# Query features of the first two batches made directly with features on partitions, and their product on quarters of the array

## The chip, the cores and the metric

The kernel runs on one core of one Trainium2 chip. The metric is device time in microseconds (us), the median of several runs; lower is better. The engines are named as in the profile: PE (TensorE products), PEld (its weight loads), DVE (VectorE), ACT (ScalarE), POOL (GpSimd) and SP (SyncE, which here issues DMAs).

## The reference

Two blocks follow each other. The first is a sketched attention over 4 batches, 4 heads, 1088 tokens and head size 32, with r = 8:

```python
def phi(x):
    a = np.einsum('rd,bhsd->bhsr', S1, x)
    b = np.einsum('rd,bhsd->bhsr', S2, x)
    return np.einsum('bhsi,bhsj->bhsij', a, b).reshape(*x.shape[:-1], r * r)
q_p, k_p = (phi(q), phi(k))
kv = np.einsum('bhsf,bhsd->bhfd', k_p, v)
z = np.sum(k_p, axis=2)
num = np.einsum('bhsf,bhfd->bhsd', q_p, kv)
den = np.einsum('bhsf,bhf->bhs', q_p, z)[..., None] + 1e-06
out = num / den
```

Every query and key of 32 numbers becomes 64 features, all products of its 8 + 8 sketches. The second block takes the 4352 tokens of 128 numbers (four heads side by side), sends each to one of 8 experts by cosine similarity with a softmax gate, and gives it that expert's two layers (128 to 1024, relu, 1024 to 128).

## The kernel before

All arithmetic is in 32-bit floating point except small counting tables. The four batches are worked on as two pairs, m = 0 and m = 1; the two batches of a pair lie side by side. Tokens come in tiles of 128; a pair has 17 tiles (the last one, the "rest", holds what is left of both batches), taken as four groups: three of 4 tiles and a last one of 4 + 1.

The order of the work is written out by hand. Each step of work is put into a numbered tick with a rank (`put(after, rank, f)`: tick of the group plus `after`), and `emit` issues all steps by tick and rank; each engine then runs its instructions strictly in that order. The keys of m = 0 take ticks 0 to 3, those of m = 1 ticks 4 to 7. The queries of m = 0 are made in ticks 0 to 3, and multiplied with the keys' sums in ticks 4 to 7; m = 1 follows in ticks 8 to 11. From tick 9 on the experts' blocks are interleaved, one a tick, with the rest of the attention and with the tables that say which token goes to which block.

What the change and the prediction touch, with the names in the code:

- `turned` (L346) turns 4 tiles of keys or queries by four products with the identity (L354) and copies the result from PSUM (L356, ScalarE). The result `kT` or `qT` has on its partitions 4 tiles x 32 head numbers, and in its columns 4 heads x 128 tokens.
- `sketch` (L362) multiplies with the block-diagonal sketch matrix `Sblk` in eight products (L371), which brings the tokens back to the partitions: the 8 + 8 sketches of every token and head. In ticks 0 to 3 keys and queries share one buffer of two PSUM banks (`ps_big`), later each has one bank (`ps_ab`).
- `second` (L375) copies one half of the sketches to SBUF (`kb`, `qb`, L377), and `features` (L380) makes the 64 products on VectorE (L383), 1024 columns for 4 tiles. For the queries of m = 0 they are kept in `held`, a part of the space of `w2_sb` that is loaded only later.
- `kv` (L420) sums keys' features times values over all tiles in PSUM (L432). At the end `total` (L438) copies the sums to SBUF: once as `kv` (L440) and twice into `kz` (L443), which holds for each pair of heads a block-diagonal 128 x 82 matrix, cleared beforehand by POOL (`clear`, L302). `tr_kv`, `kvT` and `kve` add to `kz` the sums already multiplied with the experts' directions (L447, L451, L455, L459).
- `tr_qp` (L504) is the second turn: eight more products with the identity (L508) put the queries' features on partitions, two heads x 64, and `qpT` (L512) copies them to SBUF (L514, ScalarE, 1024 columns). For m = 0 this is done one or two ticks before their use.
- `nd` (L516) multiplies `qpT` with `kz`: 16 products a group (L522), 128 rows by 64 of the array's columns, 82 moving columns, into `ps_big`. The two halves of 64 tokens go to the two halves of the array's columns.
- `x` (L529) divides by the denominator and sums the experts' parts on VectorE (L532 to L539); `squares` (L541) makes the norms on ScalarE (L544) and POOL (L546).
- `router` (L597) picks the expert and writes the tokens' rows to DRAM (`write`, L660, and on POOL L666); `fetch` (L858) gathers blocks of rows (L861), `up` and `down` are the two layers (L917, L943), with weights copied on VectorE (L874).

PSUM has two buffers of one bank (`ps_t`), two of two banks (`ps_big`), and one bank each for `ps_acc` and `ps_ab`. A step that needs a buffer waits until all readers of its last use are done. SP issues the loads in the order of the program, at most eight of them under way at a time: q, k and v of the pairs, then the experts' weights; the writes of rows and the late part of `w2_sb` follow in the same queue.

Of the kernel before, what the change touches and what calls it, by code (L numbers as in the profile page):

```python
# [19 lines left out]
P = 128  # L20
# [43 lines left out]
def kernel(  # L64
# [25 lines left out]
    def ps_big():  # L90
        return psum.tile([P, 2, 512], F32, tag="big", bufs=2, name="ps_big")
# [130 lines left out]
    nc.vector.tensor_mul(Sblk, bview(ST, [[0, H], [1, 2 * R]]), bview(mask4, [[1, H], [0, 2 * R]]))  # L222

    half_c = consts.tile([P, SPAN], F32, name="half_c")
    nc.gpsimd.memset(half_c, 0.5)
# [70 lines left out]

    kz = [consts.tile([P, 2, 2, 2, COLS], F32, name=f"kz{m}") for m in range(NM)]

    en_blk = consts.tile([P, 4, 2, E], F32, name="en_blk")

    def clear(m):
        nc.gpsimd.memset(kz[m], 0.0)  # L302

# [75 lines left out]

    def features(ab, b, n, tag, t=None):  # L380
        if t is None:
            t = tile_of(n, [P, n, H, R * R], tag)
        nc.vector.tensor_mul(t.rearrange("p j h (i k) -> p (j h) i k", i=R),  # L383
                             ab[:, :, 0].unsqueeze(3).broadcast_to([P, n * H, R, R]),
                             b.unsqueeze(2).broadcast_to([P, n * H, R, R]))
        return t

    def ab_bank(tick, n, u):


        if (tick, n) not in ab_ps:
            if tick >= 2 * n_g and n == 1:
                ps = ab_ps[tick, 4][:, 1:]
            elif n == 1:
                ps = ps_small()[:, :2 * n * HALF].rearrange("p (u n) -> p u n", u=2)
            elif tick < n_g:
                ps = ps_big()
            else:

                ps = ps_one("acc" if tick == 2 * n_g + 1 else "ab").rearrange("p (u n) -> p u n", u=2)  # L400
            ab_ps[tick, n] = ps
        return ab_ps[tick, n][:, u, :n * HALF]

    def keys(m, c0, c1, put):
# [33 lines left out]
        def total():  # L438
            s["kv"] = work.tile([P, 2, 2, D], F32, tag="kv", bufs=1, name="kv")
            nc.scalar.copy(s["kv"], acc[m][:, :, :, :D])  # L440
            for u in range(2):
                r = slice(u * HALF, (u + 1) * HALF)
                nc.scalar.copy(kz[m][r, :, :, u, :D + 1], acc[m][r, :, :, :D + 1])  # L443

# [8 lines left out]
        def kve():  # L453
# [3 lines left out]
            for u in range(2):  # L457
                r = slice(u * HALF, (u + 1) * HALF)
                nc.scalar.copy(kz[m][r, :, :, u, D + 1:], ps[r, :, :, u])  # L459
# [18 lines left out]
    def queries(m, c0, c1, put, put_nd):  # L478
# [21 lines left out]
        def prod():  # L500
            t = held[:, c0 // 4].rearrange("p (j h f) -> p j h f", j=4, h=H) if m == 0 and n > 1 else None
            s["qp"] = features(s["ab"], s["b"], n, "qp", t)

# [12 lines left out]
        def nd():  # L516
            ps = ps_big().rearrange("p b (u n) -> p (b u) n", u=2) if n > 1 else ps_small().unsqueeze(1)
            W = 2 * COLS
            for j in range(n):
                for p in range(2):  # L520
                    for i in range(2):
                        nc.tensor.matmul(  # L522
                            ps[i * HALF:(i + 1) * HALF, j, p * W:(p + 1) * W],
                            s["qpT"][:, p, j * P + i * HALF:j * P + (i + 1) * HALF],
                            kz[m][:, i if n == 1 else c0 // NK, p].rearrange("p h d -> p (h d)"), start=True, stop=True)
            s["hs"] = ps[:, :n, :2 * W].rearrange("p n (h d) -> p n h d", h=H)
            spare[m, c0] = ps[:, 0, 2 * W:]

        def x():  # L529
            hs = s["hs"]  # L530
            rc = work.tile([P, 4, H], F32, tag="rc", name="rc")[:, :n]
            nc.vector.tensor_scalar_add(rc, hs[:, :, :, D], DEN_EPS)  # L532
            nc.vector.reciprocal(rc, rc)
            nc.vector.tensor_mul(xg[g][:, own, :DM].rearrange("p n (h d) -> p n h d", h=H), hs[:, :, :, :D],  # L534
                                 bview(rc, [[H, n], [1, H], [0, D]]))

            t = work.tile([P, 4, H, E], F32, tag="parts", bufs=1, name="parts")[:, :n]
            nc.vector.tensor_mul(t, hs[:, :, :, D + 1:], bview(rc, [[H, n], [1, H], [0, E]]))
            nc.vector.reduce_sum(out=lg[g][:, own], in_=t.rearrange("p n h e -> p n e h"), axis=AX.X)  # L539

# [559 lines left out]
```

## Time and profile before

| | us |
|---|---|
| median of 9 runs | 212.23 |
| lowest and highest run | 211.31, 215.24 |
| profiled execution, whole | 211.22 |
| its span, first to last instruction | 209.3 |

The profiled execution lies about 1 us below the median. Its span is 1.9 us shorter than its whole time. The granted clock of TensorE is 1.00 in it.

Reading it: a group line gives the source line, engine, operation, tiles (out<-in), shape, then the busy time, the mean ns of one instruction and the idle time of the engine before it. A 32-bit product is recorded as two MATMUL and two LDWEIGHTS instructions; a turn as one of each. The durations of single products overlap, as they are pipelined; their rate is read from the time from the first start to the last. In the windows each row gives its stretch and length, then busy us and instruction count for PE, PEld, DVE, ACT and POOL, the granted clock, the DMA engines' share and GB/s.

The groups of the stage in question, for orientation (busy us, mean ns):

| group | count | busy | mean |
|---|---|---|---|
| L508 PE, second turn of m = 0 | 32 | 4.3 | 278 |
| L514 ACT, its copy (both pairs) | 8 | 8.1 | 1007 |
| L522 PE, features times kz (both pairs) | 256 | 10.9 | 236 |
| L371 PE, sketch of q in ticks 0 to 3 | 64 | 2.6 | 225 |
| L383 DVE, features of q, m = 0 | 4 | 4.9 | 1213 |
| L356 ACT, copy of 512 columns | 8 | 4.7 | 587 |
| L534 DVE, product of 512 columns from PSUM | 8 | 5.5 | 691 |

### The profile page before, as it was taken

To read this page: it belongs to the slowest core of one execution; us is meant where nothing else is said; L and a number is where in the kernel's file an instruction comes from. 1 tells how busy PE (TensorE), PEld (TensorE's weight loads), DVE (VectorE), ACT (ScalarE), POOL (GpSimd) and SP (SyncE) were. 2 spreads that over 40 slices of the span, in tenths; PEclk is the share of its full clock that TensorE was granted. 3 is DMA by queue.
4 is the path that set the end of the run, shared out by engine and by line. 5 is a ranking of instruction groups with operands and counts; after the bars stand their busy time and mean duration, and the time that the engine had idled before them with its cause. 6 is when DMAs were issued, how large, how long until landed. Compare 5 with 4: busy or idle time off the path is not lost.

```text
span 209.3 us, 6754 instructions
## 1 busy us (share of the span) xinstructions
PE 196.3 (94%) x2566; PEld 186.4 (89%) x2566; DVE 127.6 (61%) x368; ACT 106.0 (51%) x288; POOL 107.6 (51%) x116
## 2 busy tenths in 40 slices
PE   8979999987889999999999999999999999999991
PEld 7758889966778989998999999999999999999990
DVE  5975576898988777888554454534535356575300
ACT  2544477675569745363334535344353534676430
POOL 4101002163278786731678777676766767751322
PEclk9999999999999999999999999999999999999999
DMA  4989889999720302300111111111011121110000
GB/s 121 310 213 303 238 298 392 384 345 315 216 57 13 138 15 97 106 30 13 27 55 39 43 39 38 43 31 47 23 42 38 38 42 28 42 42 10 10 25 25
DMA packets 18369, 22.68 MB, mean 108 GB/s; under 512 B 5353, under 2 KB 12532, under 8 KB 18336
## 3 DMA queue, kind: packets, MB, share of 16 engines
q1 hardware_dynamic: 15904, 17.33, 25.2%
q0 software_dynamic: 2432, 4.90, 8.6%
q8 instruction: 22, 0.36, 0.7%
q14 instruction: 11, 0.09, 0.1%
HBM read 17.61 MB, written 4.74 MB: 107 GB/s over the span
## 4 chain that ended last, share of the span: by engine, by line
issue 32%; PE 23%; DVE 18%; POOL 15%; SPq 4%; DMA 3%; POOLq 2%; ACT 2%; DVEq 0%; ACTq 0%
POOL xs L861 9%; PE ps_big L917 6%; POOL out_dram L952 5%; DMA k_rest<-in_k_dram 3%; PE ps_acc L943 3%; SPq L125 3%; PE ps_big L522 3%; PE ps_big L508 2%; DVE wb L874 2%; DVE xg L534 2%; PE ps_acc L432 2%; PE ps_ab L943 2%; DVE qp L383 2%; PE ps_t L728 2%; DVE kp L383 1%
## 5 line engine op out<-in xcount | busy, mean ns | idle before, releaser
L952 POOL DMA_INDIRECT out_dram<-y,dst_i x36 | 49.4, 1372 | 37.4 <-ACT y L949 33.3
L917 PE MATMUL ps_big<-xTb,wb 128*128 128x128 f32 x512 | 63.1, 276 | 0.9 <-ACT xTb L870 0.4
L917 PEld LDWEIGHTS ps_big<-xTb,wb 128*128 128x128 f32 x512 | 59.7, 192 | 2.0 <-issue 1.0
L925 ACT ACTIVATE hT<-ps_big 128x1024 f32<-128x1024 f32 x36 | 36.8, 1023 | 48.1 <-PE ps_big L917 46.2
L861 POOL DMA_INDIRECT xs<-rows,src_i x36 | 37.6, 1045 | 18.9 <-issue 13.5
L874 DVE COPY wb<-w_sb 128x1024 f32 x35 | 38.6, 1104 | 11.3 <-issue 9.9
L943 PE MATMUL ps_acc<-w_sb,hT 128*128 x256 | 31.3, 275 | 0.0
L943 PE MATMUL ps_ab<-w_sb,hT 128*128 x256 | 31.2, 275 | 0.0
L943 PEld LDWEIGHTS ps_ab<-w_sb,hT 128*128 128x128 f32 x256 | 29.9, 192 | 0.0
L943 PEld LDWEIGHTS ps_acc<-w_sb,hT 128*128 128x128 f32 x256 | 29.8, 192 | 0.0
L934 DVE TENSOR_SCALAR gate<-gate 128x1 f32<-128x1 f32 x36 | 5.5, 152 | 30.3 <-ACT probs L931 30.3
L546 POOL TENSOR_TENSOR xg<-ssq,half_c 128x4 f32<-128x4 f32 (+1 forms) x10 | 9.8, 984 | 23.2 <-ACT sq L544 23.1
L870 DVE COPY xTb<-ps_t 128x128 f32<-128x128 f32 x30 | 8.7, 290 | 14.5 <-PE ps_t L867 14.3
L949 ACT ACTIVATE y<-ps_ab,gate 128x128 f32<-128x128 f32 x18 | 6.6, 367 | 12.6 <-PE ps_ab L943 11.1
L949 ACT ACTIVATE y<-ps_acc,gate 128x128 f32<-128x128 f32 x18 | 6.6, 367 | 10.4 <-PE ps_acc L943 8.8
L522 PE MATMUL ps_big<-kz,qpT 128*64 128x82 f32 x256 | 10.9, 236 | 0.9 <-issue 0.5
L522 PEld LDWEIGHTS ps_big<-kz,qpT 128*64 128x64 f32 x256 | 9.6, 136 | 2.0 <-issue 1.5
L544 ACT ACTIVATE sq<-xg 128x128 f32<-128x128 f32 x34 | 10.6, 311 | 1.2 <-DVE xg L534 0.4
L931 ACT ACTIVATE probs<-xs 128x8 f32<-128x8 f32 x36 | 10.6, 294 | 0.0
L867 PE MATMUL ps_t<-ident,xs 128*128 128x128 f32 x36 | 10.2, 283 | 0.4 <-DMA xs<-rows,src_i 0.4
L432 PE MATMUL ps_acc<-v,kp 128*64 128x64 f32 x256 | 9.2, 225 | 0.4 <-DVE kp L383 0.4
L432 PEld LDWEIGHTS ps_acc<-v,kp 128*64 128x64 f32 x256 | 8.1, 138 | 1.5 <-issue 0.8
(242 smaller groups left out, 296.1 us busy)
## 6 DMA issues: line engine op xcount, KB each, us to landing
w_sb<-in_moe_w_dram SPq DMA_DIRECT2D x32, 256.0 KB, 5.4
rows<-xg SPq DMA_DIRECT2D x4, 548.0 KB, 4.2
v<-in_v_dram SPq DMA_DIRECT2D x4, 512.0 KB, 6.0
k<-in_k_dram SPq DMA_DIRECT2D x3, 512.0 KB, 6.0
q<-in_q_dram SPq DMA_DIRECT2D x3, 512.0 KB, 5.4
xs<-rows,src_i POOLq DMA_INDIRECT x36, 2.5
out_dram<-y,dst_i POOLq DMA_INDIRECT x36, 2.8
k<-in_k_dram SPq DMA_DIRECT2D x2, 256.0 KB, 3.8
```

The lines of the kernel that those rows point to most:

```text
L432: nc.tensor.matmul(acc[m][u * HALF:(u + 1) * HALF, i, p], s["kp"][:, c - c0, h], bass.AP(tensor=vo.tensor, offset=vo.offset, ap=[list(vo.a ...
L522: nc.tensor.matmul(ps[i * HALF:(i + 1) * HALF, j, p * W:(p + 1) * W], s["qpT"][:, p, j * P + i * HALF:j * P + (i + 1) * HALF], kz[m][:, i ...
L544: nc.scalar.activation(sq, xg[g][:, at + j, :DM], ACT.Square, accum_out=ssq[g][:, at + j:at + j + 1])
L861: nc.gpsimd.indirect_dma_start(out=xs[i][:], out_offset=None, in_=rows[:2 * S if t == 0 else N], in_offset=bass.IndirectOffsetOnAxis(ap=sr ...
L867: nc.tensor.transpose(ps[:, :P], xs[i][:, :DM], ident)
L874: copy(to.rearrange("p (f q) -> p f q", f=NF), w1_sb[:, bass.ds(e, 1)].rearrange("p o (q f) -> p (o f) q", f=NF))
L917: nc.tensor.matmul(ps[:, u, j * P:(j + 1) * P], w[:, f * P:(f + 1) * P], x, start=True, stop=True)
L925: nc.scalar.activation(hT[i], ps, ACT.Relu)
L931: nc.scalar.activation(p, xs[i][:, DM:DM + E], ACT.Exp, scale=xs[i][:, ROW - 1:], accum_out=gate[i])
L943: nc.tensor.matmul(ps, h[:, f * P:(f + 1) * P], ws[0][:, f], start=f == 0, stop=f == NF - 1)
L949: nc.scalar.activation(y, ps, ACT.Copy, scale=gate.pop(i)[:, 0:1])
L952: d = nc.gpsimd.indirect_dma_start(out=out[:, :], out_offset=bass.IndirectOffsetOnAxis(ap=dst_i[t][:, j:j + 1], axis=0), in_=y[:], in_offs ...
```

## The change

For the groups of 4 tiles of m = 0, the queries' features are no longer made with tokens on partitions and then turned. Instead `S_pairs` (made once on VectorE) holds the first sketch matrix with each of its columns repeated 8 times, and the second with its 8 columns repeated as a whole, 64 columns each. `pairs` multiplies these with `qT`, 32 rows at a time (one tile's head numbers), which gives both factors of every feature with features on partitions: 16 products a group, on four row slices and two column halves of the array, into both buffers of `ps_big`. `seconds` copies the second factor to SBUF on ScalarE in two parts, and `prods` multiplies the two on VectorE in two parts, into `held`, which now has the layout of `qpT`. The sketch, `second`, `features`, `tr_qp` and `qpT` of these groups go; the rest tile and m = 1 keep them.

For both pairs, `nd` now uses 64 rows by 64 columns of the array for each product: one head at a time, 41 moving columns, 32 products a group instead of 16. `kz` holds no zero blocks any more, so it is copied once instead of twice and POOL no longer clears it. `x` reads the new layout. The keys' sketches of ticks 0 to 3 move to the single bank `ps_ab`, and the turn of the keys of m = 0 moves ahead of the queries' products.

```diff
+    S_pairs = consts.tile([P, 2, R, R], F32, name="S_pairs")
+    nc.vector.tensor_copy(S_pairs[:, 0], bview(ST, [[1, R], [0, R]]))
+    nc.vector.tensor_copy(S_pairs[:, 1], bview(ST[:, R:], [[0, R], [1, R]]))
...
-    kz = [consts.tile([P, 2, 2, 2, COLS], F32, name=f"kz{m}") for m in range(NM)]
+    kz = [consts.tile([P, 2, 2, COLS], F32, name=f"kz{m}") for m in range(NM)]
...
-            elif tick < n_g:
-                ps = ps_big()
             else:
...
-            for u in range(2):
-                r = slice(u * HALF, (u + 1) * HALF)
-                nc.scalar.copy(kz[m][r, :, :, u, :D + 1], acc[m][r, :, :, :D + 1])
+            nc.scalar.copy(kz[m][:, :, :, :D + 1], acc[m][:, :, :, :D + 1])
...
-        put(-1, 52, tr)
+        put(-1, 49.9 if m == 0 and n > 1 else 52, tr)
...
-        put(0, 47.9 if ahead else 50.1, b)
+        put(0, 47.9 if ahead else 49.85, b)
...
+        def pairs():
+
+            s["big"] = ps_big(), ps_big()
+            for t in range(2):
+                for u in range(2):
+                    for j in range(4):
+                        r = slice(j * D, (j + 1) * D)
+                        nc.tensor.matmul(s["big"][j // 2][u * HALF:(u + 1) * HALF, j % 2, t * 2 * P:(t + 1) * 2 * P],
+                                         S_pairs[r, t].rearrange("p i k -> p (i k)"),
+                                         s["qT"][r].rearrange("p (a u n) -> p a u n", a=2, u=2)[:, :, u],
+                                         start=True, stop=True)
+
+        def seconds(j):
+            if j == 0:
+                s["b"] = tile_of(n, [P, 2, w], "qpT")
+                s["qpT"] = held[:, c0 // 4].rearrange("p (a n) -> p a n", a=2)
+            nc.scalar.copy(s["b"][:, j].rearrange("p (j n) -> p j n", j=2), s["big"][j][:, :, 2 * P:])
+
+        def prods(j):
+            nc.vector.tensor_mul(s["qpT"].rearrange("p a (j n) -> p j a n", j=4)[:, 2 * j:2 * j + 2],
+                                 s["big"][j][:, :, :2 * P].rearrange("p j (a n) -> p j a n", a=2),
+                                 s["b"][:, j].rearrange("p (j a n) -> p j a n", j=2, a=2))
...
-            ps = ps_big().rearrange("p b (u n) -> p (b u) n", u=2) if n > 1 else ps_small().unsqueeze(1)
-            W = 2 * COLS
+
+            ps = ps_big()
             for j in range(n):
                 for p in range(2):
                     for i in range(2):
-                        nc.tensor.matmul(
-                            ps[i * HALF:(i + 1) * HALF, j, p * W:(p + 1) * W],
-                            s["qpT"][:, p, j * P + i * HALF:j * P + (i + 1) * HALF],
-                            kz[m][:, i if n == 1 else c0 // NK, p].rearrange("p h d -> p (h d)"), start=True, stop=True)
+                        for u in range(2):
+                            r = slice(u * HALF, (u + 1) * HALF)
+                            nc.tensor.matmul(
+                                ps[i * HALF:(i + 1) * HALF, u, (2 * j + p) * COLS:(2 * j + p + 1) * COLS],
+                                s["qpT"][r, p, j * P + i * HALF:j * P + (i + 1) * HALF],
+                                kz[m][r, i if n == 1 else c0 // NK, p], start=True, stop=True)
...
-            put(0, 50, ab)
-            put(0, 50.5, b)
-            put(0, 54, prod)
-            for i, f in enumerate((tr_qp, qpT)):
-                put_nd(*((0, 47.7 + 0.02 * i) if c0 == 0 else (-1, 57)), f)
+            if n == 1:
+                put(0, 50, ab)
+                put(0, 50.5, b)
+                put(0, 54, prod)
+                for f in (tr_qp, qpT):
+                    put_nd(-1, 57, f)
+            else:
+                put(0, 50, pairs)
+                for j in range(2):
+                    put(0, 50.5, lambda j=j: seconds(j))
+                    put(0, 54, lambda j=j: prods(j))
...
-    put_at(1)(0, 91, lambda: clear(0))
-    put_at(2)(0, 91, lambda: clear(1))
```

The second part of `kve` is copied to `kz` in the new layout too, and `x` takes its slices of `hs` and its reciprocals with the heads as two factors; both keep their numbers of elements.

More of the change, by code (lines that the diff above doesn't have):

```diff
@@ L294, in iotas @@
         nc.vector.tensor_copy(digits, tok_i[:, 1:])
-    kz = [consts.tile([P, 2, 2, 2, COLS], F32, name=f"kz{m}") for m in range(NM)]
+    kz = [consts.tile([P, 2, 2, COLS], F32, name=f"kz{m}") for m in range(NM)]
     en_blk = consts.tile([P, 4, 2, E], F32, name="en_blk")
-    def clear(m):
-        nc.gpsimd.memset(kz[m], 0.0)
     emb_of = {}
@@ L378, in second, with features @@
         return b
-    def features(ab, b, n, tag, t=None):
-        if t is None:
-            t = tile_of(n, [P, n, H, R * R], tag)
+    def features(ab, b, n, tag):
+        t = tile_of(n, [P, n, H, R * R], tag)
         nc.vector.tensor_mul(t.rearrange("p j h (i k) -> p (j h) i k", i=R),
@@ L458, in kve @@
                 r = slice(u * HALF, (u + 1) * HALF)
-                nc.scalar.copy(kz[m][r, :, :, u, D + 1:], ps[r, :, :, u])
-        put(-1, 52, tr)
+                nc.scalar.copy(kz[m][r, :, :, D + 1:], ps[r, :, :, u])
+        put(-1, 49.9 if m == 0 and n > 1 else 52, tr)
         ahead = m == 1 and c0 == 0
         put(0, 47.8 if ahead else 49.8, ab)
-        put(0, 47.9 if ahead else 50.1, b)
+        put(0, 47.9 if ahead else 49.85, b)
         put(0, 53, prod)
@@ L500, in prod @@
         def prod():
-            t = held[:, c0 // 4].rearrange("p (j h f) -> p j h f", j=4, h=H) if m == 0 and n > 1 else None
-            s["qp"] = features(s["ab"], s["b"], n, "qp", t)
+            s["qp"] = features(s["ab"], s["b"], n, "qp")
+        def pairs():
[17 more added lines that the diff above has]
+                                 s["b"][:, j].rearrange("p (j a n) -> p j a n", j=2, a=2))
         def tr_qp():
@@ L521, in nd @@
                     for i in range(2):
-                        nc.tensor.matmul(
-                            ps[i * HALF:(i + 1) * HALF, j, p * W:(p + 1) * W],
-                            s["qpT"][:, p, j * P + i * HALF:j * P + (i + 1) * HALF],
-                            kz[m][:, i if n == 1 else c0 // NK, p].rearrange("p h d -> p (h d)"), start=True, stop=True)
-            s["hs"] = ps[:, :n, :2 * W].rearrange("p n (h d) -> p n h d", h=H)
-            spare[m, c0] = ps[:, 0, 2 * W:]
+                        for u in range(2):
[4 more added lines that the diff above has]
+                                kz[m][r, i if n == 1 else c0 // NK, p], start=True, stop=True)
@@ L529, in x @@
+            s["hs"] = ps[:, :, :2 * n * COLS].rearrange("p u (n a d) -> p n a u d", n=n, a=2)
+            spare[m, c0] = ps[:, 0, 8 * COLS:]
         def x():
             hs = s["hs"]
-            rc = work.tile([P, 4, H], F32, tag="rc", name="rc")[:, :n]
-            nc.vector.tensor_scalar_add(rc, hs[:, :, :, D], DEN_EPS)
+            rc = work.tile([P, 2, 8], F32, tag="rc", name="rc")[:, :, :2 * n].rearrange("p u (n a) -> p n a u", n=n)
+            nc.vector.tensor_scalar_add(rc, hs[:, :, :, :, D], DEN_EPS)
@@ L533, in x @@
             nc.vector.reciprocal(rc, rc)
[L534 to L539, printed above, removed]
+            nc.vector.tensor_mul(xg[g][:, own, :DM].rearrange("p n (a u d) -> p n a u d", a=2, u=2), hs[:, :, :, :, :D],
+                                 rc.unsqueeze(4).broadcast_to([P, n, 2, 2, D]))
@@ L541, in squares @@
+            t = work.tile([P, 4, 2, 2, E], F32, tag="parts", bufs=1, name="parts")[:, :n]
+            nc.vector.tensor_mul(t, hs[:, :, :, :, D + 1:], rc.unsqueeze(4).broadcast_to([P, n, 2, 2, E]))
+            nc.vector.reduce_sum(out=lg[g][:, own], in_=t.rearrange("p n a u e -> p n e (a u)"), axis=AX.X)
         def squares():
```

## The prediction

> **What bounds the kernel now.** I read the page's busy shares first, then the chain of waits, then VectorE's idle times and the stages by windows.
>
> ```profile
> PE 196.3 (94%) x2566; PEld 186.4 (89%) x2566; DVE 127.6 (61%) x368; ACT 106.0 (51%) x288; POOL 107.6 (51%) x116
> ```
>
> TensorE is busy almost throughout, so products taken away should count; where they count is told by the chain of waits in the stage that the change touches:
>
> ```profile
> 21.45 1.84 PE ps_acc L432 x48
> 23.28 1.02 PE ps_big L508 x8
> ...
> 26.00 0.88 PE ps_big L508 x8
> ...
> 26.92 1.36 PE ps_big L522 x32
> 28.28 0.46 PE ps_ab L371 x16
> 28.75 0.59 PE ps_t L354 x4
> 29.34 1.08 PE ps_acc L432 x32
> 30.42 1.02 PE ps_big L508 x8
> 31.44 1.29 PE ps_big L522 x32
> ```
>
> From 21.45 to 37.9 us TensorE alone makes the chain, and the second turns of the queries (L508) stand in it. VectorE meanwhile waits for L522, three times (its timeline; in brackets the idle time before the instruction):
>
> ```profile
> 28.32 0.17 DVE L532 TENSOR_SCALAR rc<-ps_big 128x16 f32<-128x16 f32 x1 [1.26 <-PE ps_big L522]
> 32.78 0.17 DVE L532 TENSOR_SCALAR rc<-ps_big 128x16 f32<-128x16 f32 x1 [1.52 <-PE ps_big L522]
> 37.90 0.17 DVE L532 TENSOR_SCALAR rc<-ps_big 128x16 f32<-128x16 f32 x1 [0.61 <-PE ps_big L627]
> ```
>
> From 37.9 to 47.7 it waits for nothing. The windows (after the span: busy us of PE, PEld, DVE, ACT, POOL) say the same:
>
> ```profile
> 28.30:32.80 4.50, 4.50 (x101) 4.03 (x98) 2.85 (x7) 3.26 (x11) 1.04 (x1) 1.00 0.96 357
> 32.80:37.90 5.10, 5.10 (x106) 4.51 (x103) 4.18 (x13) 3.70 (x13) 1.01 (x1) 1.00 1.05 388
> 37.90:48.00 10.10, 9.29 (x203) 8.11 (x204) 9.47 (x29) 7.31 (x29) 4.50 (x5) 1.00 0.99 353
> 48.00:59.60 11.60, 8.96 (x153) 7.54 (x149) 10.04 (x36) 5.16 (x11) 4.05 (x5) 1.00 0.75 230
> 59.60:112.00 52.40, 51.14 (x529) 49.34 (x530) 38.81 (x123) 28.44 (x89) 34.54 (x32) 1.00 0.17 53
> ```
>
> So: TensorE to 37.9, VectorE and its chain to the first block at 59.6, TensorE again from there. A shift of VectorE's start at 37.9 moves all that follows; a shorter product counts again from 59.6.
>
> **Prices.** The rows for products, from the groups and the timeline:
>
> ```profile
> L917 PE MATMUL ps_big<-xTb,wb 128*128 128x128 f32 x512 | 63.1, 276 | 0.9 <-ACT xTb L870 0.4 <-DVE gate L934 0.2 <-DVE wb L874 0.2
> 26.92 1.36 PE L522 MATMUL ps_big<-kz,qpT 128*64 128x82 f32 x32
> 67.93 0.24 PE L522 MATMUL ps_t<-kz,qpT 128*64 128x82 f32 x2
> 75.11 0.24 PE L753 MATMUL ps_big<-total,ones 128*128 128x8 bf16 x4
> ```
>
> Each f32 product is two instructions. L917's 16 take 2.02 us with the last one's 0.276: (2.02-0.276)/15 = 0.116 us for 128 columns, 0.91 ns a column with the whole array. L522's 32, writing either half of the array's columns in turn, start every (1.36-0.236)/31 = 0.036 us, where 82 columns alone would cost 0.075: two go side by side, and the pair at 67.93 starts within about 10 ns. No row shows products that share the array by rows.
>
> *pairs* (new): 16 products, 32 instructions of 256 columns, 0.233 each alone. Eight abreast it is 0.93 us, two abreast 3.7, one by one 7.5. I take 1.0, because the halves by columns, the nearest row, do run fully abreast.
> *nd* (changed): 64 instructions of 41 columns at 0.037. Four abreast 0.6 us; two abreast 1.19, about today's 36 x 32 = 1.15. L753's four start every (0.24-0.166)/3 = 0.025 us; if that bounds every start, 1.6. I take 0.8, nearer to L522's starts side by side than to L753's, which share one place: 0.35 saved a call.
>
> Against the nd part speaks the Trainium skill, "TensorEngine Tiling (Array Packing)", Instruction Overhead: a product of 1 column lasts as long as one of 60, so no tiling factor should be drawn from a dimension that is already small. By that rule 82 columns made 41 bring almost nothing: an estimate from its 60 cycles is 1.6 us one after another, L753's bound again. For the pairs speaks "TensorE: Matmul & The Clock Gate", Part 3: row tiles start about 4 ns apart, and four with 32 rows gained 3.07 times; times two column halves, an estimate of 7.5/6.1 = 1.2 us for pairs. L753's row agrees with the first page in its size; the second no run here shows.
>
> **The change, part by part.**
> *Ticks 0 to 3 (to 23.3 us).* Removed per tick: the sketch of q (L371, 16 instructions, 0.46), its copy qb (0.27), the product L383 (1.21). Added: pairs 1.0, two copies of 512 columns (row of qT: 0.59 each), two VectorE products of 512 columns from PSUM (row of L534: 0.69 each, 1.38 in all). The S_pairs copies cost VectorE 2 x 0.22 (row of L222) while its constants hold it until 8.33; its first kp moves to 8.7. The new wait: pairs need both buffers of ps_big, so pairs of one tick start after the last prods of the one before: pairs 1.0, latency 0.2, copy 0.6, two prods 1.4, 0.2 of hand-overs: about 3.4 us a tick. Behind the waiting pairs stand on TensorE the next q's turn and kv. The keys' sketch now has one buffer (ps_ab) for two, but kp frees it before the pairs loop comes round. By these rows pairs(0) start at 7.8, prods(0) end at 11.3, pairs(1) start at 11.4, pairs(2) at 14.8. Today TensorE stands idle 1.3 us until the k_rest load lands at 16.0; that idle time covers part. From 14.8 TensorE has pairs(2) 1.0, kv(0) 1.1, the turns 0.8, kv(1) 1.1, sketch(3) 0.7, pairs(3) 1.0, rest and k turn 0.8, kv(2) 1.1, kv(3) with its rest 1.8: 24.2, less 0.2 where they overlap, against 23.28 now: 0.7 late. VectorE's kp(3) comes 0.6 later too (emb_sq stands behind two more ScalarE copies).
> *Tick 4.* L508 goes twice (1.02 and 0.88), as does the ScalarE copy L514 (1.02) and one of three kz copies. What is late next is kv, turn, kvT, en product, kz copies: 0.3 + 0.3 + 0.3, the sketch and k turn between (1.1), the en product 0.3, kz 0.4: about 2.6 after 24.0. The first nd starts at 26.6 against 26.92: 0.3 won. With the shorter nd VectorE's first x starts 0.65 earlier.
> *Tick 5.* Today x to x is 32.78 - 28.32 = 4.46 us, TensorE's. L508 leaves (0.88 of its 1.02; the change of shape costs about 0.14 as now) and nd shrinks by 0.35: 3.23. VectorE's own work there is x 1.72 and kp 1.22, 2.94, so TensorE still leads narrowly. Won: 1.23.
> *Tick 6.* VectorE has x, best and pick, kp: 4.5 of 5.12 us; the third L508 set and the 0.61 idle go, and VectorE is next. Won: 0.6. At 37.9 the gain is 0.65 + 1.23 + 0.6 = 2.5.
> *From there to 59.6* VectorE's work is unchanged and carries it. Loads come in time: q of the second pair is issued by 24.5 with 5.4 us to landing and first turned at 38.5; w1 is issued by 41.6 and first read at 55.4; w2's late part is wanted at 68.7. held is now freed by nd instead of the second turn, but its reload stands in SP's queue behind the write of rows at 44.6, as today.
> *From 59.6* two nd of the second pair lie in TensorE's full stretch: 2 x 0.35 = 0.7, less 0.1 for the last rest.
> The cleared kz memsets (2 x 0.37) lay in POOL's idle time: nothing. x reads as many elements as before, in another order: nothing, with 0.1 to either side from its 0.69. The last rest's nd moves to a ps_big buffer that x has freed by then (39.8 against 41.2 today): nothing.
> Sum: 2.5 + 0.6 = 3.1 us. The profiled execution took 211.2 (span 209.3): 208.1 for it. The runs' median is 212.2, 1.0 above it: I forecast 212.2 - 3.1 = 209.1.
> With nd at 0.6 and TensorE's kv not late at all it is 3.9 + 0.7 = 4.6: 207.6.
>
> **Rivals.**
> *A, starts bound nd (1.6 us).* For: L753's 0.025. Against: the 10 ns at 67.93. First x 0.15 later, tick 5 wins 0.4, tick 6 0.6, the late nds lose 0.9: 212.3, no change.
> *B, slower: the eight do not run abreast.* Place: pairs, on TensorE in front of kv and inside the loop above. Two at a time 3.7 us: 2.7 more in each of three rounds, 8.1 later at kv(3), less 3.1: 217. It decides from pairs of 2.0 us upward (3 x 1.0 eats the gain). For: no row shows row sharing; u changes slowest but one in its loop, so column halves alone would hardly pair. Against: four different banks, 32-row slices each with its own weights.
> *C, the early start is given back.* The first fetch at 56.3 follows POOL's row writes of 51.1 with 4.6 to landing. If the loads, DMA share 0.99 then, hold those writes, only the late nd counts: 0.6, 211.6.
>
> **How the numbers follow.** Forecast 0.69, A 0.13, B 0.14, C 0.04. The range leaves out B and little below: from 207.4 to 212.8. A measurement here can tell about 0.3% from no change (0.6 us): faster 0.70, same 0.15, slower 0.15.
>
> **What would show it.** L508 on w_sb gone; pairs from first start to last end at about 1.2 us; nd's 64 starts in 0.8; VectorE's idle times of 1.52 and 0.61 gone; the x that stood at 37.9 at about 35.4; the first L917 at about 57.1. Pairs above 2 us, or a kv(3) that ends after 25 us, would make it wrong.

## The result and the profile after

The changed kernel takes 215.78 us (median of 10 runs, 213.74 to 216.78); the kernel before, on the same chip, 212.22 (31 runs). The ratio is 1.016, with a 95% interval of 1.0131 to 1.0189: slower by some 3.5 us, where 3.1 us less was forecast. The ratios leave out runs that count as slow (over 1.5% above the fastest of their kernel), so a ratio need not be the quotient of the two medians. The profiled execution took 213.53 us (span 211.7), 0.2 under the lowest of the timed runs. Against the profile before, it is 2.4 us longer in span, so the profiles show 2.4 of the 3.5 us.

The page's first part, as in the prediction:

```profile
PE 196.6 (93%) x2870; PEld 185.2 (87%) x2870; DVE 127.9 (60%) x374; ACT 105.0 (50%) x286; POOL 108.1 (51%) x114
```

TensorE is as busy as before (196.6 against 196.3 us) with 304 more MATMUL and 304 more LDWEIGHTS records: nothing was taken from it in sum. TensorE's timeline (start, us, engine, line, tiles, count, and in brackets the idle time before and what ended it) shows where the time went:

```profile
8.11 1.12 PE L506 MATMUL ps_big<-qT,S_pairs 32*64 32x256 f32 x32
...
26.79 1.34 PE L542 MATMUL ps_big<-kz,w_sb 64*64 64x41 f32 x64 [0.64 <-ACT kz L455]
...
30.35 0.89 PE L542 MATMUL ps_big<-kz,w_sb 64*64 64x41 f32 x42
33.93 0.55 PE L542 MATMUL ps_big<-kz,w_sb 64*64 64x41 f32 x22 [2.69 <-issue]
...
35.73 1.93 PE L430 MATMUL ps_acc<-v,kp 128*64 128x64 f32 x32
...
38.21 1.58 PE L542 MATMUL ps_big<-kz,w_sb 64*64 64x41 f32 x64
...
44.04 0.45 PE L542 MATMUL ps_big<-kz,w_sb 64*64 64x41 f32 x17 [0.66 <-issue]
```

Up to the first nd all is about as predicted: the first pairs (L506) are done in 1.1 us and the first nd stands at 26.79 (forecast 26.6). This nd takes as long as before (1.34 us here, 1.36 there). Then the second nd breaks off **in the middle of a run of like products**: after 42 of its 64 TensorE stands for 2.69 us, and "issue" says that it waited for nothing that the profile shows. No product that the change adds or removes has this duration. Afterwards kv takes 1.93 us where the same row takes 1.15 at 29.27. The windows give the granted clock (the number before the DMA share):

```profile
28.30:32.80 4.50, 2.94 (x94) 2.52 (x90) 2.75 (x6) 2.36 (x10) 1.05 (x1) 1.00 0.96 329
32.80:37.90 5.10, 3.97 (x77) 3.54 (x77) 3.05 (x12) 2.35 (x11) 0.00 (x0) 0.80 1.04 391
...
32.40:35.81 3.41, 1.88 (x45) 1.59 (x47) 1.20 (x4) 0.35 (x2) 0.35 (x1) 1.00 1.06 399
35.81:39.22 3.41, 3.41 (x74) 2.96 (x74) 3.03 (x9) 2.55 (x11) 1.02 (x1) 0.50 1.02 371
39.22:42.63 3.41, 3.41 (x113) 3.04 (x110) 2.35 (x7) 1.45 (x6) 0.00 (x0) 1.00 0.98 342
```

The 0.80 is a mean: behind the hole the clock is 0.50 from 35.81 to 39.22 us and 1.00 before and after. VectorE's x shows what both cost:

```profile
28.20 0.19 DVE L552 TENSOR_SCALAR rc<-ps_big 128x16 f32<-128x16 f32 x1 [1.23 <-PE ps_big L542]
34.54 0.19 DVE L552 TENSOR_SCALAR rc<-ps_big 128x16 f32<-128x16 f32 x1 [3.39 <-PE ps_big L542]
40.18 0.18 DVE L552 TENSOR_SCALAR rc<-ps_big 128x16 f32<-128x16 f32 x1 [1.10 <-PE ps_big L653]
```

The x that stood at 37.90, and was to stand at 35.4, stands at 40.18. From there on little is won or lost: x stands 2.3 us later than before, the first block's first layer starts at 61.89 against 59.66 (+2.2), the span ends at 211.7 against 209.3 (+2.4).

**Where the holes lie.** The DMA queues in the window from 27 to 34 us (packets, MB, share of the 16 engines):

```profile
q1 hardware_dynamic: 1422, 2.15, 89.4%
q8 instruction: 1, 0.02, 0.9%
```

One packet of 16 KB on the instruction queue lies among the loads. By the trace's packet times it ran from 31.53 to 32.55, and TensorE resumed at 33.93. The page counts 24 such packets after and 22 before, for 6116 and 5504 TensorE records (products, weight loads and the sequencer's own, such as waits): about one for 256 records. Counted that way, the holes of all kernels below stand at records 449, 705, 1217, 1473 and 1729 (and, in e9, one at 6593), always 256 or a multiple of it apart. So I take the packets for TensorE's own next page of instructions. The table is read from packet and record times; "asked" is the moment at which TensorE passes the edge of the page before (the request is inferred, not recorded), "256 in" is how long TensorE needs for that page's 256 records. The hole is counted here from start to start, so it is about 0.2 us longer than the idle time in the lines above (2.92 and 2.69).

| kernel | asked at | landed after | 256 in | hole at the next edge | TensorE resumes after landing |
|---|---|---|---|---|---|
| before | 30.07 | 4.00 | 6.71 | none | |
| after | 27.42 | 5.13 | 3.60 | 2.92 | 1.38 |
| after | 39.38 | 3.16 | 3.77 | 0.89 | 1.50 |
| e1 | 16.86 | 5.47 | 5.57 | 1.38 | 1.48 |
| e2 | 29.23 | 5.47 | 4.70 | 2.21 | 1.44 |
| e5 | 29.78 | 2.04 | 3.53 | none | |
| e5 | 33.32 | 5.16 | 4.01 | 2.77 | 1.63 |
| e8 | 41.71 | 3.22 | 4.41 | 0.25 | 1.44 |
| e13 | 28.04 | 5.06 | 3.60 | 2.76 | 1.30 |
| e15 | 27.91 | 2.98 | 5.31 | none | |

In the profiles of before, after and the eighteen kernels below there are 26 holes of over 0.3 us at a page's edge, and each ended 1.2 to 1.6 us after its page had landed. **A hole is landing time plus about 1.4 us, less the time of 256 instructions.** Given the 1.4 us, this is arithmetic; what it says of the chip is that the 1.4 us hardly changes (1.2 to 1.6), and that up to 60 us no edge stayed without a hole where the rule asks for one of over 0.4 us. The change raised TensorE's records in a tick from 184 to 232 from tick 4 on (16 fewer for the second turn, 64 more for nd), and in the stretch of the second nd 256 records went in 3.6 us instead of 6.7.

### The profile page after: what moved, and what is told of

Same layout as the page of the kernel before. It is cut to its first block, busy times and chain, and to the rows that moved or that the text cites. A ratio compares the mean times of both kernels' runs of the same rounds, so it can differ in the third digit from the quotient of the medians.

```text
span 211.7 us, 7363 instructions
## 1 busy us (share of the span) xinstructions
PE 196.6 (93%) x2870; PEld 185.2 (87%) x2870; DVE 127.9 (60%) x374; ACT 105.0 (50%) x286; POOL 108.1 (51%) x114
## 4 chain that ended last, share of the span: by engine, by line
PE 33%; issue 32%; POOL 14%; DVE 13%; ACT 3%; POOLq 2%; DMA 1%; DVEq 0%; ACTq 0%
POOL xs L887 9%; PE ps_big L943 7%; POOL out_dram L978 5%; PE ps_acc L430 4%; PE ps_t L355 3%; PE ps_big L542 3%; PE ps_acc L969 3%; PE ps_ab L969 3%; PE ps_big L506 2%; PE ps_ab L372 2%; PE ps_acc L103 2%; PE ps_t L754 2%; DVE xg L554 2%; DMA xs<-rows,src_i 1%; DVE wb L900 1%
## 5 line engine op out<-in xcount | busy, mean ns | idle before, releaser
L978 POOL DMA_INDIRECT out_dram<-y,dst_i x36 | 50.1, 1391 | 36.2 <-ACT y L975 31.1
L951 ACT ACTIVATE hT<-ps_big 128x1024 f32<-128x1024 f32 x36 | 36.9, 1024 | 47.8 <-PE ps_big L943 45.9
L887 POOL DMA_INDIRECT xs<-rows,src_i x36 | 38.3, 1065 | 18.9 <-issue 13.7
L900 DVE COPY wb<-w_sb 128x1024 f32 x35 | 38.6, 1103 | 11.7 <-issue 10.3
L383 DVE TENSOR_TENSOR kp<-ps_ab,kb 128x1024 f32<-128x1024 f32 x8 | 9.7, 1216 | 3.0 <-ACT qpT L515 2.4
L430 PEld LDWEIGHTS ps_acc<-v,kp 128*64 128x64 f32 x256 | 8.9, 148 | 1.5 <-issue 1.1
L430 PE MATMUL ps_acc<-v,kp 128*64 128x64 f32 x256 | 10.0, 236 | 0.0
L542 PE MATMUL ps_big<-kz,w_sb 64*64 64x41 f32 x256 | 5.7, 240 | 4.0 <-issue 3.4
```

Of the source, the lines that this page charges most:

```text
L430: nc.tensor.matmul(acc[m][u * HALF:(u + 1) * HALF, i, p], s["kp"][:, c - c0, h], bass.AP(tensor=vo.tensor, offset=vo.offset, ap=[list(vo.a ...
L542: nc.tensor.matmul(ps[i * HALF:(i + 1) * HALF, u, (2 * j + p) * COLS:(2 * j + p + 1) * COLS], s["qpT"][r, p, j * P + i * HALF:j * P + (i + ...
L887: nc.gpsimd.indirect_dma_start(out=xs[i][:], out_offset=None, in_=rows[:2 * S if t == 0 else N], in_offset=bass.IndirectOffsetOnAxis(ap=sr ...
L900: copy(to.rearrange("p (f q) -> p f q", f=NF), w1_sb[:, bass.ds(e, 1)].rearrange("p o (q f) -> p (o f) q", f=NF))
L951: nc.scalar.activation(hT[i], ps, ACT.Relu)
L978: d = nc.gpsimd.indirect_dma_start(out=out[:, :], out_offset=bass.IndirectOffsetOnAxis(ap=dst_i[t][:, j:j + 1], axis=0), in_=y[:], in_offs ...
```

## The experiments

Theory F: the time is lost to pages that come late behind the loads. Rival G: the new forms (quarters of the array, or the pairs) cost the time by themselves. Each ratio is to the kernel before on the same chip; that kernel's median lay between 211.86 and 214.92 from one series of runs to the next (214.92 and 212.50 on one and the same chip).

### Halves of the change: e1 (pairs alone), e2 (quarters alone)

```diff
 e1: the changed kernel, but in nd, kz, x
-  64 rows x 64 columns, 41 streamed, 32 products a group
+  128 rows x 64 columns, 82 streamed, 16 products a group (as before)
 e2: the kernel before, but with the quarters' nd, kz and x
```

> The changed kernel with the features' product, kz and its clearing as before (16 products a group, 82 columns); only the pairs are kept. Theory, late instructions: the product on quarters doubles TensorE's instructions per tick just while the weights' loads fill the DMA engines, and TensorE runs out of instructions; here the hole of 2.7 us inside a product at 31 us is gone, the clock stays 1.00, VectorE's x that stood at 37.9 us stands at 35.5 to 36.5, and the time is 209.5 to 211. Rival, the pairs themselves (their row slices, or the buffers they hold) make the loss: the time stays at 214 or above.

> The kernel before with only the features' product on quarters of the array, with its kz; the second turn stays. Late instructions: 248 instructions a tick instead of 184, so holes of 1 to 3 us without a waiting engine appear between 26 and 45 us, and the time is 213 to 217. Rival, pairs make the loss: no hole, 211.5 to 212.5.

e1: 217.68 us, ratio 1.0145 (1.0041 to 1.0249). Missed: it was to be faster. The hole in the second nd went, but two others came at earlier edges, both in kv (0.76 and 1.16 us of idle time; TensorE's timeline of e1 shows the second):

```profile
23.81 1.79 PE L433 MATMUL ps_acc<-v,kp 128*64 128x64 f32 x54 [1.16 <-issue]
```

TensorE of e1 also waits 2.10 us for the first fetched rows, up to 61.24 us, and the clock is 0.50 from 63.22 to 66.63. e2: 223.4 us over runs of 216.82 to 224.57, too far apart for an interval; its profile (of an execution of 222.41) has holes of 0.80, 2.21 and 1.48 us, start to start. So neither half is free of holes. Their places speak for F (the same records), their mere presence in e1 does not tell F from G.

### Smaller loads: e3 (after), e4 (before)

```diff
-        for u in range(2):   # each weight load 256 KB
+        for u in range(4):   # 128 KB
```

> The changed kernel with each load of the experts' weights cut from 256 KB to 128 KB; eight loads are under way at a time, so half as many bytes stand in front of an instruction page. Late instructions: the hole shrinks to 0 to 1.3 us and the time falls to 210 to 213. Rival, the product on quarters is slow in itself or stalls on data: the hole stays at 2.5 us or above and the time at 215 to 216.5.

> Control: the kernel before with the same halved loads. Late instructions: before had few holes, so 211.5 to 212.7. If the loads' size matters for another reason (first fetch, rows), it moves by more than 1 us here as well.

e3: 230.25, ratio 1.0682 (1.0585 to 1.0779); e4: 222.42, 1.0336 (1.0225 to 1.0446). The hole in the second nd shrank to 1.21 us of idle time, and its page landed after 3.72 us, as F has it. The totals tell nothing of pages: more issues in SP's queue put the writes of rows and the first fetch off. In TensorE's timeline of e3 the first turn of a fetched block waits for its rows (the number in brackets):

```profile
72.02 0.48 PE L893 MATMUL ps_t<-ident,xs 128*128 128x128 f32 x1 [11.57 <-DMA xs<-rows,src_i]
```

and in e4 by 6.33 us.

### Loads held back: e5 (after), e6 (pairs), e7 (before)

```diff
+    def paced(n, after):
+            nc.gpsimd.tensor_scalar_add(to[0:1, 0:1], after, 0.0)
             nc.sync.dma_start(to, src)
+            put(-1, 52.01, lambda: paced(3, s["kT"][0:1, 0:1]))
+            put(0, 53.01, lambda: paced(3, s["kp"][0:1, 0, 0, 0:1]))
```

> The change with one thing else: the 24 early loads of w1 and w2 don't go out in one row; three at a time wait for the second pair's kT or kp (a tiny POOL write into each load's target makes them wait), so at most some 0.8 MB of them stand in the queues instead of 2 MB and more. Theory F (TensorE's next page of 256 instructions comes late behind the weight loads, and TensorE resumes about 1.45 us after it lands): the page asked for at about 27.4 us lands within 3 us instead of 5.1, so of the 2.7 us hole in the second nd at most 0.9 is left; the granted clock stays at 0.98 or more from 32 to 38 us; the x that stood at 40.2 stands at 38.2 or earlier; the whole is 2 to 3 us under the changed kernel, about the time before. Rival G (quarters of the array stop TensorE by themselves, or the products wait for something that the trace does not name): the hole of 2.7 us and the low clock after it stay, and the time stays at 1.016 of before. Both: if the later loads come too late, VectorE's wb copies or the first L943 wait for a DMA; then only the stage up to 48 us counts.

> The pairs alone (nd, kz and x as before), with the same paced loads as in e5. Theory F: the second of the two early holes (1.2 us at 23.8, asked for at 16.9) stays or shrinks a little, as it stands behind the loads of the second pair's k, v and q and not behind weights; from 26 us on there is no hole, each 256 instructions take 5.3 us or more there. Time about 1.5 us under the pairs alone without pacing, between 0.995 and 1.01 of before. Rival G': the pairs themselves cost what e1 lost (1.45%), and pacing leaves that: 1.012 or more.

> The kernel before with the paced loads, the control of e5 and e6. Theory F: its 256 instructions take 6.7 to 7.2 us in the stage of the loads and the pages 4.0 us at most, so there is no hole to remove: 0.997 to 1.003 of before. Rival: pacing helps or harms by itself (the writes of rows get through sooner or later): then e5 and e6 are to be read against this one.

e5: 217.47, ratio 1.0267 (1.0229 to 1.0305): the total missed. The hole in the second nd went altogether, as its page landed after 2.04 us, and came back one page on, where the page took 5.16 (TensorE's timeline of e5; two smaller ones, 0.44 and 1.38, lie in the first 24 us):

```profile
32.71 1.14 PE L554 MATMUL ps_big<-kz,w_sb 64*64 64x41 f32 x64
...
36.55 1.01 PE L554 MATMUL ps_big<-kz,w_sb 64*64 64x41 f32 x50
40.10 0.44 PE L554 MATMUL ps_big<-kz,w_sb 64*64 64x41 f32 x14 [2.55 <-issue]
```

The same code runs through in one place and stands still in the next: that is against G. e5 loses time later as well: TensorE waits 2.03 us for the first fetched rows, and the clock is 0.50 from 65.42 to 68.83. e6: 212.87 (210.35 to 215.06), ratio 0.999 (0.9934 to 1.0046), profiled span 208.5 with no hole above 0.4; the profiled execution is its lowest run, 0.7 us under the lowest of before. e7: 212.80, ratio 1.0063 (1.0024 to 1.0102), 0.7 us above what was expected; its early page came late (1.38 us).

### More instructions, no quarters: e8

```diff
 (kernel before, nd of the first pair)
+            for _ in range(32):
+                nc.tensor.matmul(ps[:16, 3, 2 * W:2 * W + 1], zeros[:, :16], zeros[:, :1], start=True, stop=True)
```

> The kernel before with 32 products of one column and 16 weight columns (zeros, into an unused corner of PSUM) behind each of the first pair's four full nd products: 128 more instructions in each of the ticks 4 to 7, no product on rows' quarters. Theory F: the padding takes about 1 us a call, 312 instructions go through in some 5.5 us, so 256 take 4.5 and a page that lands 4 to 5 us after it was asked for leaves a hole of 1 to 2 us, at a page's edge (256 instructions apart from the ones seen: record 1217 or 1473), with no wait named. Rival G: no hole over 0.3 us besides those of before, as nothing here uses the array by rows.

218.65 us (one run). Missed in size: the padding took 1.75 us a call, not 1, and pages landed after 2.0 to 3.8 us from 24 us on, so one hole of 0.25 us came where 1 to 2 were expected (another, of 0.83 us, stands at 24.0 us, ahead of any padding). By the rule above it should be 3.22 + 1.4 - 4.41 = 0.2. It fits F but is too small to decide.

### The products by themselves: e9

```diff
+        for t in range(32):   # after the last block; six such loops on zeros
+            nc.tensor.matmul(ps[(column half), u, :41], zeros[(row half), :HALF], wide[(row half), :41], start=True, stop=True)
```

> The changed kernel with six rows of 32 f32 products of zeros behind TensorE's last work, each on its own line: (1) halves, 64 weight columns, 82 streamed, as nd before; (2) quarters, 64 weight columns, 41 streamed, as nd now; (3) quarters, 82 streamed; (4) quarters, 32 weight columns, 41 streamed; (5) quarters, 64 weight columns, 8 streamed; (6) halves, 41 streamed. If the load of 64 weight columns is what bounds nd (four in 58 ns, row 2), rows 2, 3 and 5 last alike, 1.1 us for 64 instructions, row 4 lasts half of it, and row 6 is as long as row 2 for as many products, or as half as many. If the streamed columns bound it, row 5 is a fifth and row 3 twice of row 2. If each start costs a fixed 17 ns, rows 2 to 6 all last alike. The time of the whole says nothing (some 8 us of added work).

TensorE's timeline behind the last block, four of the six rows:

```profile
211.82 2.49 PE L1086 MATMUL ps_big<-wide,zeros 128*64 128x82 f32 x64
214.24 1.14 PE L1088 MATMUL ps_big<-wide,zeros 64*64 64x41 f32 x64
215.20 1.34 PE L1090 MATMUL ps_big<-wide,zeros 64*64 64x82 f32 x64
...
218.65 1.11 PE L1094 MATMUL ps_big<-wide,zeros 64*64 64x8 f32 x64
```

In single starts: two halves with 82 streamed columns go every 71 ns, four quarters with 41 every 58, with 82 every 71, with 8 every 58, and with 32 weight columns (41 streamed) mostly every 36. Two halves with 41 streamed columns (the sixth row) go every 58 too, until the clock falls to 0.50 at 220.47. Neither fixed reading holds alone: in these rows a set of products side by side lasts as long as **the larger of its weight columns and its streamed columns**, 0.87 to 0.91 ns each. Products that share one place have a floor besides: those that pad e8, with 16 weight columns and one streamed, start every 25 ns where this reading would give 15. nd has 16 sets before and after, so quarters save 16 x 13 ns = 0.21 us, not 0.35. At the end of this run, with the DMA engines nearly idle, a page landed after 1.99 us while 256 records went in 2.01, and the hole was 1.39: the rule gives 1.38. In the kernel even nd's 0.21 is lost at the two changes of shape: the steps at nd's head (80 and 129 ns) and tail (157) stand outside its sets, so that 1.28 us pass from its first start to the next product.

### No early weights: e10 (after), e11 (before), e12 (pairs)

```diff
-            nc.sync.dma_start(w1_sb[...], w1[...])    # 24 loads
+    put_at(1)(0, 92, lambda: fill([w1_sb[:, e] for e in range(E)], E))         # nc.gpsimd.memset
+    put_at(2)(0, 92, lambda: fill([w2_sb[:, e] for e in range(E // 2)], E // 2))
```

> The changed kernel with the 24 early loads of w1 and w2 left out (6 MB); POOL fills those tiles with 0.01 in its idle time instead, so the experts' products read no weights and the output isn't the reference's, while the instructions of TensorE stay. Theory F: from about 30 us on pages land within 2 us of being asked for, no hole over 0.3 us at a page's edge after that, the clock at 1.00; nd to nd in the next tick takes 3.35 us as in the paced run; the x that stood at 40.2 stands at 36.3 or earlier; the time lies 1 to 2 us (0.990 to 0.995) under the kernel before with the same loads left out. Rival G (the quarters themselves cost the time): it stays 1.0% or more above that control.

> The kernel before with the same loads left out and filled: the control of the two others. Theory F: its holes were 0.1 us and less in the profiled run, so it gains under 0.5 us against the kernel before, 0.997 to 1.000. Rival: the loads held the kernel before as well (its writes of rows and the first fetch): 0.990 or less, and then a gain of the changed kernel by leaving them out is not about pages alone.

> The pairs alone (nd as before) with the same loads left out and filled. Theory F: as nd in quarters lasts as long as nd before (1.34 against 1.36 us), this one is as fast as the changed kernel without loads, within 0.3%: the whole gain, 1 to 2 us under the control, is the second turns'. Rival: the quarters bring 0.35 us a call after all once nothing holds TensorE: then it is 1 us or more slower than the changed kernel without loads.

The medians are 216.61 us (e10, ratio 1.0179, 1.0081 to 1.0277), 215.76 (e11, 1.0168, 1.0064 to 1.0271) and 217.1 (e12, 213.36 to 219.4, no interval): e10 and e12 are not under their control e11, and e11 is above before, so the totals missed what was expected. The totals are spoilt by the filling: beside POOL's 12 fills (11.7 us in e10) small VectorE instructions of the first 28 us took longer, one of them 3.27 us in e11 that takes 0.28 in the changed kernel. The stage behind them counts: between 36 and 50 us e10's pages landed after 1.8 to 2.0 us, no hole was left, and x followed x after 3.36 and 4.45 us (VectorE's timeline of e10),

```profile
37.01 0.19 DVE L550 TENSOR_SCALAR rc<-ps_big 128x16 f32<-128x16 f32 x1 [1.23 <-PE ps_big L540]
40.37 0.19 DVE L550 TENSOR_SCALAR rc<-ps_big 128x16 f32<-128x16 f32 x1 [0.41 <-PE ps_big L540]
44.82 0.18 DVE L550 TENSOR_SCALAR rc<-ps_big 128x16 f32<-128x16 f32 x1
```

against 4.46 and 5.12 in e11 and 3.28 and 4.43 in e12. **These are the predicted ticks** (3.23 and 4.5), and the pairs alone bring all of it.

### One expert's weights: e13 (after), e14 (before), e15 (pairs)

```diff
-    for e in range(E):            # 24 loads
+    (e = 0 only: 4 loads)
+    w1_one = bview(w1_sb[:, 0], [[0, E], [1, F]])    # every expert reads expert 0
+    w2_one = bview(w2_sb[:, 0], [[0, E], [DM, NF], [1, DM]])
```

> The changed kernel with the early weights of one expert only (4 loads, 1 MB, in place of 24, 6 MB); all blocks use this expert's weights, so the output isn't the reference's, but every product and copy stays, and no engine does any filling. Theory F: pages land within 2.5 us of being asked for from 30 us on, no hole over 0.3 us at a page's edge there, clock 1.00; x to x 3.35 us in tick 5 and 4.45 in tick 6; the x that stood at 40.2 stands at 36.3; the time is 1.5 to 2 us below the kernel before with one expert's weights (ratio of the two 0.990 to 0.993). Rival G (something else in the change holds the later stages): the ticks shorten but the two times are within 0.5 us of one another, or the changed one is slower.

> The kernel before with one expert's early weights: the control. Theory F: it had no late page from 24 us on in the profiled run, so 0.993 to 1.000 of before. Rival: the weights' loads hold it elsewhere too (writes of rows, first fetch): 0.99 or less.

> The pairs alone (nd as before) with one expert's early weights. Theory F and the bench of nd (four quarters go every 58 ns, two halves every 71, and the change of shape costs about 0.2 us a call): within 0.4 us of the changed kernel with one expert's weights. Rival: quarters bring 0.35 us a call, then 1 us or more above it.

| | median (runs) | ratio to before | profiled span |
|---|---|---|---|
| e13, after | 212.80 (12) | 1.0007 (0.9974 to 1.0041) | 211.3 |
| e14, before | 210.43 (11) | 0.9904 (0.9873 to 0.9935) | 208.5 |
| e15, pairs | 209.52 (6) | 0.9861 (0.9815 to 0.9907) | 206.1 |

e15, without quarters, comes close to the forecast. VectorE's timeline has its x,

```profile
28.25 0.17 DVE L555 TENSOR_SCALAR rc<-ps_big 128x16 f32<-128x16 f32 x1 [1.51 <-PE ps_big L545]
31.54 0.17 DVE L555 TENSOR_SCALAR rc<-ps_big 128x16 f32<-128x16 f32 x1 [0.35 <-PE ps_big L545]
35.97 0.17 DVE L555 TENSOR_SCALAR rc<-ps_big 128x16 f32<-128x16 f32 x1
```

and TensorE's the first block's first layer:

```profile
57.12 2.05 PE L946 MATMUL ps_big<-xTb,wb 128*128 128x128 f32 x16 [0.35 <-ACT xTb L899]
```

35.97 (forecast 35.4) and 57.12 (forecast 57.1; the control e14 has 59.54). That the second meets the forecast to 0.02 us is luck: x is 0.57 late, and from x to the first layer e14 and e15 take 21.2 us where before takes 21.8. e13 differs from e15 in nd, kz and x alone, and its page landed after 5.06 us with a sixth of the weights in the queues, against my 2.5 (TensorE's timeline of e13):

```profile
34.40 0.55 PE L542 MATMUL ps_big<-kz,w_sb 64*64 64x41 f32 x22 [2.54 <-issue]
```

One page on it has another, of 0.73 us, and x stands at 40.20, not at 36.3. Its windows around the first hole:

```profile
29.79:33.21 3.42, 2.07 (x76) 1.78 (x74) 1.95 (x4) 2.10 (x9) 0.89 (x1) 1.00 0.94 335
33.21:36.62 3.41, 2.22 (x57) 1.94 (x59) 1.50 (x5) 0.69 (x2) 0.16 (x1) 1.00 0.45 133
```

So the part of theory F that blames the weights alone falls; the late page stays, and with it the DMA share of 0.94 up to 33.21 us from the loads that are left. e13's total is what rival G said: 2.4 us above its control, where 1.5 to 2 below was expected. Its spans say where: x is 1.8 us behind e14's, less than the two holes come to, and some 1.0 us more is lost behind x, which nothing here explains. The quarters' 64 added records a call decide between e13 and e15: at 5.3 us for 256 the pairs bear a page of 3.9 us, at 3.6 us only one of 2.2; but e15's page came sooner as well (2.98 us), so part of the difference is the page's. By the profiles e15 gains 2.4 us on e14, but its profile is of its lowest run and e14's of a middle one; by the medians it is 0.9, and their intervals overlap.

### Holding back from the start: e16 (pairs), e17 (pairs), e18 (before)

```diff
 e16: also the second pair's later k, v and its q through paced(), 2 to 4 a gate
 e17, e18: one gate for all of these loads and the weights
+        nc.gpsimd.tensor_scalar_add(k_sb[1][0:1, 0, NK, 0:1], after, 0.0)   # after: third kp
```

> The pairs alone, nd as before, and all loads that are not wanted before 30 us (the second pair's later k and v, its q, and the early weights) sent out two to four at a time, each group when a kT or kp of the second pair is written. Theory F: the page asked for at 16 to 17 us lands 3.5 us later or sooner, so the early hole at a page's edge (1.38 us in e1) goes in most runs, and the time is that of the undisturbed run of e6, 210.5, in more of the runs: 0.990 to 0.996 of before. Rival: the writes of rows and the first fetch come behind the later loads, and the first block starts later: 1.005 or more, with the wait for the first fetch in VectorE's or TensorE's rows at 58 to 62 us.

> The pairs alone, nd as before, with one gate in SP's queue: the second pair's later k and v, its q and all early weights go out, in their old order, only when the first pair's third kp is written (about 18 us; one tiny POOL write into the first of these loads' targets makes it wait). Theory F: the page asked for at 16 us lands within 3.5 us, so there is no hole at the early page's edge (1.38 in e1); the loads then end about 3 us later than in e1, early enough for the writes of rows; 0.990 to 0.996 of before, and under e18. Rival: as in e16 the loads still fill the queues when rows are written and fetched: a wait for the first fetch of 1 us or more, and 1.005 of before or more.

> The kernel before with the same gate, the control of e17. Theory F: its early page hole (0.1 us in the profiled run, 0.5 to 1.4 in other kernels with the same first ticks) goes, its later stages have no late page: 0.995 to 1.000 of before. Rival: the later loads hold the first fetch: 1.005 or more.

e16 and e17 were tries at a version that beats both kernels, and neither does; e18 is the control of e17. e16: 215.52, ratio 1.0146 (1.0098 to 1.0195). From the second on its pages landed after 1.8 to 3.9 us, there was no hole and x stood at 36.26, but what the rival said came true: SP issued weights until 46.4 us and the first rows only at 46.8 (44.6 before). TensorE's timeline of e16 shows the wait for the first fetched rows and the low clock behind it

```profile
60.81 0.47 PE L915 MATMUL ps_t<-ident,xs 128*128 128x128 f32 x1 [3.84 <-DMA xs<-rows,src_i]
61.64 3.79 PE L965 MATMUL ps_big<-xTb,wb 128*128 128x128 f32 x16 [0.35 <-ACT xTb L918]
```

(3.79 us for what takes 2.04 at the full clock). e17: 216.07, ratio 1.0202 (1.0147 to 1.0258), for a reason that neither theory named: the gated k load was issued at 26.50, behind weight loads, and TensorE waited 5.59 us for it. e18: 211.68, ratio 0.9995 (0.9955 to 1.0034), no hole, no gain.

## Why the prediction was wrong, step by step

- **Pairs 1.0 us, ticks 0 to 3:** right. 1.1 to 1.4 us, eight abreast (in the first pairs eight starts 6 to 7 ns apart, the next eight some 0.2 us later; later ones less evenly); kv(3) ends at 23.9 (24.0), the first nd starts at 26.79 (26.6). Rival B did not happen.
- **nd 0.8 us, 0.35 saved a call:** wrong. From first to last of its starts it takes 1.12 us, before 1.13 (1.34 and 1.36 with the last one's end). I priced starts. What counts is the 64 weight columns of each set (58 ns, e9), and the change of shape eats the rest. The first x came 0.12 earlier, not 0.65, and the late nds brought nothing of 0.7. The Trainium skill's "TensorEngine Tiling (Array Packing)", Instruction Overhead, had spoken against this: 8 streamed columns indeed last as long as 41 in e9 (58 ns a set). But it is the 64 weight columns that set this: with 32 of them a set takes 36 ns. Rival A (1.6 us) erred to the other side: its 25 ns a start hold for products that share one place (e8), not for these.
- **Tick 5 won 1.23:** the step that failed. x to x took 6.34 us instead of 3.23. Some 2.9 us of that is the late page, which no term of my sum and no rival held; I counted starts and columns and put the delivery of the instructions at nothing, without a reason. Where the pages come in time the tick takes 3.28 to 3.36 (e10, e12, e15).
- **Tick 6 won 0.6:** right in e10, e12 and e15 (4.43 to 4.45); in the changed kernel it took 5.64, since kv, L526 and nd fell into the 3.41 us at the clock of 0.50 (0.78 + 0.25 + 0.24 us more). The third of the waits that I put down to L522, the 0.61 us, was ended by L627 behind it.
- Summed, x at 40.18 less 35.4 forecast is 4.8 us: 0.5 from nd, 3.1 in tick 5, 1.1 in tick 6 (0.1 are roundings).
- **From 37.9 to 59.6 VectorE carries it on:** right, 21.7 us after and 21.8 before, which is why the loss reaches the end whole. Rival C did not happen in the changed kernel, but the first fetch came late in e3, e4 and e16 (11.57, 6.33 and 3.84 us of waiting), and by 1.3 to 2.1 us in e1, e2 and e5.

The Trainium skill's "Runtime: NRT & Kernel Launch", Instruction fetch mechanics, describes blocks of 256 instructions in 16 KiB, which agrees with the packets here, and calls the cost of crossing a block's edge mostly hidden. In this stage the runs differ: 2.9 and 0.9 us at two crossings of the changed kernel.

**Open:** what makes a page land after 2 us in one case and 5 in another with like loads (e13 and e15 at 28 us: 5.06 and 2.98). Loads have to do with it: in e10, with a DMA share of 0.35 from 36 to 50 us, pages land after 1.8 to 2.0 us; but e13's next page, asked for at 34.40, took 3.50 us with a share of 0.49. Open is also how far the spread of the timed runs (213.74 to 216.78 after), and the 1.1 us that the medians show beyond the profiles, are holes, since only one execution of each has a trace. Half open is why the clock falls after some holes and not others. Before a trace's last microseconds each fall is to 0.50, for one or more stretches of 3.41 us on a grid that is fixed within the trace. Where the stretch in which a hole ended had TensorE busy for 34 to 55% (e9, e5, e2, the changed kernel: 55%), the next ran at 0.50; e13's hole of 2.54 us lies across two stretches, 61 and 65% busy, and the clock stayed at 1.00. That this share decides is read off, not tested, and elsewhere there are exceptions: e12 stayed at 1.00 after 46% (from 25.55 us), e3 and e10 fell after 79% (from 51.64 and 57.00).

## What to carry to other kernels

Count TensorE's instructions by the time, not only its columns: a 32-bit product is four records here, and where 256 records take less than the page's landing time (2.0 to 6.5 us at the 26 holes here) plus 1.4 us, TensorE stands still with no wait named. By e9, splitting a product into smaller ones side by side pays only as far as the larger of weight and streamed columns shrinks. A gap inside a run of like products, ended by "issue", is to be looked for at the packets of the instruction queue.

## What the runs showed of the hardware

- Pages of 16 KB, one for 256 TensorE records; late ones cost 0.25 to 3.3 us, each hole ending 1.2 to 1.6 us after its page had landed (26 holes over 0.3 us).
- The granted clock falls to 0.50 for whole stretches of 3.41 us: from 35.81 to 39.22 us in the changed kernel, behind a stretch in which TensorE was busy for 1.88 of 3.41 us.
- Products on 32-row slices times column halves do run eight abreast (e15's pairs as well as the changed kernel's); four quarters every 58 ns with 64 weight columns, 36 with 32.
- Beside POOL's fills of 1024 columns (about 1 us each) VectorE's small instructions took up to 3 us longer (e10, e11).
- A load that was gated (e17) was issued behind weight loads that follow it in the program, and cost TensorE 5.59 us.
